# A quarter-block of the output weights in six partitions at a time: one change to a cached grouped-query attention kernel

## The chip, the cores and the metric

The kernel runs on one core of a Trainium2 chip. A core has a matrix engine (TensorE, PE in the profile), three engines for element work (VectorE or DVE, ScalarE or ACT, GpSimd or POOL), a queue engine that here issues nearly all transfers (SyncE, SP), and sixteen DMA engines that move data between the chip's main memory and the on-chip memory SBUF, whose tiles have up to 128 partitions. TensorE writes its products into a second memory, PSUM. The metric is the device time of one execution in microseconds (us), taken as the median of several runs.

## What is computed

One block of attention over a cache, for 8 sequences of 4 new tokens each, 32 query heads that share 8 key/value heads, 2048 cached positions and heads of 128:

```python
q = (x @ wq).reshape(B, Sq, Hq, Dh).transpose(0, 2, 1, 3)
k = jnp.repeat(k_cache, rep, axis=1)
v = jnp.repeat(v_cache, rep, axis=1)
scores = jnp.einsum("bhqd,bhkd->bhqk", q, k) * (Dh ** -0.5)
p = softmax(scores, axis=-1)
o = jnp.einsum("bhqk,bhkd->bhqd", p, v)
return o.transpose(0, 2, 1, 3).reshape(B, Sq, Hq * Dh) @ wo
```

All arrays are bfloat16. The two caches are 32 MB each (8 x 8 x 2048 x 128), wq and wo 4 MB each, x and the result 32 KB.

## The kernel before

**Units and steps.** Two key/value heads of one sequence make a unit: 32 units (`NU`), ordered by head pair `p` (0 to 3) and sequence `b` (0 to 7). A unit's K and V are one transfer of 1 MB each (`load_k` L92, `load_v` L102), 128 partitions with 8 KB in a row. A unit is worked on in two halves, so there are 64 steps (`NH`), and the loop runs ahead by `L` = 6 steps: in one pass it transposes K of the half-unit `step + 7` on TensorE (`transpose_part`, L199), forms the scores of `step + 6` (`scores`, L217) with the exponential on ScalarE (L227), and sums the values of `step` (`values`, L241). At the first half of a unit `norms` sums the exponentials on TensorE (L255), VectorE reduces them and takes the reciprocal (L263, L267); at the second half `finish` multiplies the unit's values by it (L272). The order of every engine's instructions is the order of the program text.

**Projection.** The result needs the product with wo, which is cut into four quarters of 1024 rows, one for each head pair `p`. When a pair is done, `to_tokens(p)` (L284, L290) turns its outputs so that tokens lie in partitions, and `to_wo_rows(p)` (L299, L304) turns them back in the order in which wo lies in SBUF: eight consecutive rows of wo (`WR` = 8) in each of 128 partitions, so that a partition gets 8 KB in a row. For quarters 0 to 2 this happens in the first units of the next pair, quarter 0's in steps 18 and 20. `project(p, r0, n)` (L309) multiplies, `2 n` products of 128 rows by 256 columns, into two PSUM tiles `out_ps`, one for each half of the 512 output columns. Quarter 0 is projected in step 59 (`NH - 5`), after that step's values; the first half of quarter 1 in step 61; the rest after the loop: `to_tokens(3)`, second half of quarter 1, `to_wo_rows(3)`, quarter 2, quarter 3 in three pieces. Then two copies and two stores.

**Loads.** SP issues all loads, in the order of the list `loads`: wq, x, then K of unit `u` and V of unit `u - 3` in turn, with wo's quarter 0 (1 MB) behind V29 and half of quarter 1 (512 KB) behind V30. V31 follows, and behind it the rest of wo in five transfers of 512, 1024, 512, 256 and 256 KB. A load waits for its buffer (7 for K, 6 for V) and for the landing of the load eight places before it, whose semaphore it uses again. `wo_sb` takes the place of `wq_sb`, which is used up by 18 us.

Of the kernel before, what the change touches and what calls it, by code (L numbers as in the profile page):

```python
# [8 lines left out]
BF16 = mybir.dt.bfloat16  # L9
# [5 lines left out]
def kernel(  # L15
# [9 lines left out]
    nc = tc.nc  # L25

    B, Sq, D = x.shape
# [4 lines left out]
    T = B * Sq  # L32
    R = D // 128
    G2 = Hkv // 2
# [3 lines left out]
    HP = 2 * rep  # L38
    scale = float(Dh) ** -0.5
    NU = G2 * B  # L40
    NH = 2 * NU
    KB = 7
    VB = 6
    L = 6
    KA = L // 2 + 1
    WR = HP
    DH = D // 2
# [5 lines left out]
    const = ctx.enter_context(tc.tile_pool(name="const", bufs=1))  # L53
    wpool = ctx.enter_context(tc.tile_pool(name="wpool", bufs=1))
    kpool = ctx.enter_context(tc.tile_pool(name="kpool", bufs=KB))
    vpool = ctx.enter_context(tc.tile_pool(name="vpool", bufs=VB))
# [5 lines left out]
    psum_l = ctx.enter_context(tc.tile_pool(name="psum_l", bufs=1, space=bass.MemoryType.PSUM))  # L62
# [11 lines left out]
    pick = const.tile([128, 2, 2, Dh // 2], BF16, name="pick")  # L74
    ident4 = const.tile([128, 128], FP32, name="ident4")
    oT_all = const.tile([128, Hq, B, Sq], BF16, name="oT_all")
    out_sb = [const.tile([T, DH], BF16, name=f"out_sb{i}") for i in range(2)]
    oP = [const.tile([128, WR, T], BF16, name=f"oP{p}") for p in range(G2)]
    ident = const.tile([128, 128], BF16, name="ident")
    ones = const.tile([128, 128], BF16, name="ones")  # L80
    probs = [const.tile([128, C, NQ], BF16, name=f"probs{i}") for i in range(L // 2 + 2)]
# [15 lines left out]
    def load_v(u):  # L97
# [6 lines left out]
            v_cache[b, 2 * p : 2 * p + 2].rearrange("g (s c) d -> (g s) c d", c=C),  # L104
        )

    def load_wo(p, r0, n):
        rows = wo[p * HP * 128 : (p + 1) * HP * 128, :].rearrange("(q r) j -> q r j", r=WR)
        nc.sync.dma_start(wo_sb[:, p, r0 : r0 + n, :], rows[:, r0 : r0 + n, :])

    nc.sync.dma_start(wq_sb[:, :, :], wq.rearrange("(p r) n -> p r n", r=R))  # L111
    nc.sync.dma_start(x_sb[:, :], x.flatten_outer_dims())  # L112
    loads = []
    for u in range(NU + KA):
        if u < NU:
            loads.append(("k", u))
        if u >= KA - 1 and u - KA + 1 < NU:
            loads.append(("v", u - KA + 1))
        if u in (NU, NU + 1):
            loads.append(("wo", (u - NU, 0, WR if u == NU else 4)))  # L120
    loads.reverse()

    def load_ready(nk, nv):

        while loads:
            kind, u = loads[-1]
            if kind == "wo":
                loads.pop()
                load_wo(*u)
                continue  # L130
            if u >= (nk + KB if kind == "k" else nv + VB):
                return
            loads.pop()
            (load_k if kind == "k" else load_v)(u)

    load_ready(0, 0)

    make_identity(nc, ident[:])
    make_identity(nc, ident4[:])
    for e in range(2):  # L140
        for g in range(2):
            nc.vector.tensor_copy(
                out=pick[:, e, g, :], in_=ident[:, :].rearrange("d (k e) -> d e k", e=2)[:, e, :]
# [2 lines left out]
    nc.vector.memset(ones[:, :], 1.0)  # L146
    for t in probs:
        nc.vector.memset(t[:, :, :], 0.0)

    for r in range(R):  # L150
        xtp = psum_o.tile([128, T], BF16, tag="o", name="xtp")
# [4 lines left out]
    for p in range(G2):  # L156
        psq = psum_s.tile([128, HP, T], FP32, tag="s", name="psq")
        for h in range(HP):
            hh = p * HP + h
            for r in range(R):  # L160
                nc.tensor.matmul(  # L161
                    psq[:, h, :],
                    lhsT=wq_sb[:, r, hh * 128 : (hh + 1) * 128],
                    rhs=xT_sb[:, r, :],
                    start=(r == 0),
                    stop=(r == R - 1),
                )
        nc.scalar.mul(  # L168
            out=qT_all[:, p, :, :, :],
            in_=psq[:, :, :].rearrange("d h (b s) -> d b h s", b=B),  # L170
            mul=scale,
        )
    for p in range(G2):
        pse = psum_s.tile([128, 2, B, NQ], FP32, tag="s", name="pse")
        for e in range(2):
            nc.tensor.matmul(  # L176
                pse[:, e, :, :],
                lhsT=pick[:, e, :, :],
                rhs=qT_all[:, p, :, :, :].rearrange("d b h s -> d (b h s)"),
                start=True,  # L180
                stop=True,
            )
        for g in range(2):
            rows = slice(g * 64, (g + 1) * 64)
            (nc.scalar.copy if g else nc.vector.tensor_copy)(  # L185
                out=q_bd[rows, p, :, :, g, :], in_=pse[rows, :, :, :]
            )

    wo_sb = wpool.tile([128, G2, WR, D], BF16, tag="w", name="wo_sb")
    kt = {}  # L190

    def transpose_part(i, part):
        u, hf = divmod(i, 2)
        c0 = hf * HC + part * (HC // 2)
        kp = psum_k.tile([128, HC // 4, 128], FP32, tag="k", name="kp")
        k4 = ks[u][:, :, :].rearrange("s c d -> s (c d)").bitcast(FP32)
        for j in range(HC // 4):
            w = (c0 // 2 + j) * 128
            nc.tensor.transpose(kp[:, j, :], k4[:, w : w + 128], ident4[:, :])  # L199
        kp2 = kp[:, :, :].rearrange("k j s -> k (j s)").bitcast(BF16)  # L200
        k_t = ktpool.tile([128, HC // 4, 128, 2], BF16, tag="kt", name="kt")
        kt2 = k_t[:, :, :, :].rearrange("k j s e -> k (j s e)")
        if part == 1 and hf == 1:
            nc.scalar.copy(out=kt2, in_=kp2)  # L204
        else:
            nc.vector.tensor_copy(out=kt2, in_=kp2)  # L206
        kt[(i, part)] = k_t

    def scores(i):
        u, hf = divmod(i, 2)  # L210
        p, b = units[u]
        pr = probs[u % len(probs)]
        s_ps = psum_s.tile([128, HC, NQ], FP32, tag="s", name="s_ps")
        for j in range(HC // 2):
            k_t = kt[(i, j // (HC // 4))]
            for e in range(2):
                nc.tensor.matmul(  # L217
                    s_ps[:, 2 * j : 2 * j + 2, :],
                    lhsT=k_t[:, j % (HC // 4), :, e],
                    rhs=q_bd[:, p, e, b, :, :],  # L220
                    start=(e == 0),
                    stop=(e == 1),
                )
        for g in range(2):
            rows = slice(g * 64, (g + 1) * 64)
            cols = slice(g * NQ // 2, (g + 1) * NQ // 2)
            nc.scalar.activation(  # L227
                out=pr[rows, hf * HC : (hf + 1) * HC, cols], in_=s_ps[rows, :, cols], func=EXP
            )
# [21 lines left out]
    def norms(u):  # L251
        pr = probs[u % len(probs)]
        l_ps = psum_l.tile([128, LC, NQ], FP32, tag="l", name="l_ps")
        for c in range(0, C, LC):
            nc.tensor.matmul(  # L255
                l_ps[:, :, :],
                lhsT=ones[:, :],
                rhs=pr[:, c : c + LC, :],
                start=(c == 0),
                stop=(c + LC == C),  # L260
            )
        l_sb = small.tile([128, NQ], FP32, tag="l_sb", name="l_sb")
        nc.vector.tensor_reduce(  # L263
            out=l_sb[:, :], in_=l_ps[:, :, :].rearrange("d c q -> d q c"), axis=AX, op=ADD
        )
        r_sb = small.tile([128, NQ], FP32, tag="r_sb", name="r_sb")
        nc.vector.reciprocal(r_sb[:, :], l_sb[:, :])  # L267
        r_sbs[u] = r_sb
# [10 lines left out]
    nats = {}  # L279
# [14 lines left out]
        nats[p] = nat_sb  # L294

    def to_wo_rows(p):
        perm = psum_l.tile([128, WR, T], BF16, tag="l", name="perm")
        for r in range(WR):
            nc.tensor.transpose(  # L299
                perm[:, r, :],  # L300
                nats[p][:, :, :].rearrange("t q r -> t r q")[:, r, :],
                ident[:T, :T],
            )
        nc.vector.tensor_copy(out=oP[p][:, :, :], in_=perm[:, :, :])  # L304

    def project(p, r0, n):
        for half in range(2):
            for r in range(r0, r0 + n):
                nc.tensor.matmul(  # L309
                    out_ps[half][:, :],  # L310
                    lhsT=oP[p][:, r, :],
                    rhs=wo_sb[:, p, r, half * DH : (half + 1) * DH],
                    start=(p == 0 and r == 0),
                    stop=(p == G2 - 1 and r == WR - 1),
                )

    for step in range(-L - 1, NH):
        i, j = step + L + 1, step + L
        if i < NH:
            transpose_part(i, 0)  # L320
        if 0 <= j < NH:
            scores(j)
        if i < NH:
            transpose_part(i, 1)
        u, hf = divmod(step, 2)
        if step >= 0:
            p, b = units[u]
            if hf == 0:
                norms(u)
            values(step)  # L330
            if hf == 1:
                finish(u)
            elif p > 0 and b == 1:
                to_tokens(p - 1)
            elif p > 0 and b == 2:
                to_wo_rows(p - 1)
        load_ready(min((i + 1) // 2, NU), max((step + 1) // 2, 0))
        if step == NH - 1 - 2 * VB:
            assert not loads
            load_wo(1, 4, 4)  # L340
            load_wo(2, 0, WR)
            load_wo(3, 0, 4)
            load_wo(3, 4, 2)
            load_wo(3, 6, 2)
        if step == NH - 5:
            out_ps = [
                psum_s.tile([T, DH], FP32, tag="s", name=f"out_ps{n}") for n in range(2)
            ]
            project(0, 0, WR)
        elif step == NH - 3:  # L350
            project(1, 0, 4)

    to_tokens(3)
    project(1, 4, 4)
    to_wo_rows(3)
    project(2, 0, WR)
    project(3, 0, 4)
# [37 lines left out]
```

The softmax here doesn't subtract the row's maximum and nothing guards it: scores larger than these inputs give would overflow.

## Time and profile before

| what | value |
|---|---|
| median of 8 runs | 192.63 us (192.37 to 193.01) |
| the profiled execution | 192.61 us |
| its span, first to last instruction | 190.8 us |
| TensorE busy | 153.9 us, 81% |
| VectorE, ScalarE, GpSimd busy | 113.4, 86.2 and 1.1 us |
| read from main memory | 75.53 MB, 396 GB/s over the span |
| K and V transfers, issue to landing | 20.3 us each (median of 32 and 32) |
| projection L309 | 64 products, 7.6 us busy |
| K transposes L199 | 512, 80.6 us busy, 10.9 us idle before them until K landed |

The span leaves out what lies around the program's instructions; 1.8 us here. TensorE's matrix products are pipelined, so a product's own duration (272 ns for L309) is longer than its distance to the next.

### The profile page before, as it was taken

What the parts mean: (1) busy time and instruction counts of PE and PEld (TensorE: products, weight loads), DVE (VectorE), ACT (ScalarE), POOL (GpSimd) and SP (SyncE); (2) the same over time, 40 slices, a digit from 0 to 9 for tenths busy, and PEclk for the clock granted to TensorE, in tenths of its full rate; (3) what the DMA queues carried; (4) which work ended last, traced back from release to release, by engine and by line L of the source; (5) the groups of instructions that cost most, each with busy time, mean ns of one, the idle gap of its engine ahead of it and who ended that gap; (6) DMA issues with size and microseconds to landing.
All of it is one profiled execution on the core that took longest, in us unless ns stands there. A gap on an engine that the chain in (4) does not pass through costs nothing.

```text
span 190.8 us, 6460 instructions
## 1 busy us (share of the span) xinstructions
PE 153.9 (81%) x2892; PEld 139.3 (73%) x2892; DVE 113.4 (59%) x220; ACT 86.2 (45%) x170; POOL 1.1 (1%) x8
## 2 busy tenths in 40 slices
PE   0018867999999999978888889998886999998783
PEld 0007657899999988867778778887775988886572
DVE  6402754677677777756665667676664477673420
ACT  2003665656665654455553444454553555451000
POOL 2000000000000000000000000000000000000000
PEclk9999999999999999999999999999999799999999
DMA  6999999999999999999999999999999999999950
GB/s 220 440 405 421 421 419 417 426 416 419 419 416 417 421 419 417 419 426 412 423 419 423 417 416 417 421 417 424 414 419 421 417 426 416 414 426 411 406 201 9
DMA packets 10539, 75.97 MB, mean 398 GB/s; under 512 B 1200, under 2 KB 1296, under 8 KB 1936
## 3 DMA queue, kind: packets, MB, share of 16 engines
q1 hardware_dynamic: 10464, 75.55, 95.6%
q8 instruction: 22, 0.36, 0.8%
q14 instruction: 5, 0.04, 0.1%
q10 hardware_dynamic: 48, 0.02, 0.0%
HBM read 75.53 MB, written 0.03 MB: 396 GB/s over the span
## 4 chain that ended last, share of the span: by engine, by line
DMA 95%; PE 2%; SPq 1%; issue 0%; ACT 0%
DMA k_sb<-in_k_cache_dram 86%; DMA wo_sb<-in_wo_dram 9%; PE out_ps L309 2%; SPq L92 1%; SPq L112 0%; SPq L111 0%; ACT out_sb L362 0%
## 5 line engine op out<-in xcount | busy, mean ns | idle before, releaser
L199 PE MATMUL kp<-ident,k_sb 128*128 128x128 f32 x512 | 80.6, 283 | 10.9 <-DMA k_sb<-in_k_cache_dram 10.9
L206 DVE COPY kt<-kp 128x1024 bf16<-128x1024 bf16 x96 | 65.2, 684 | 27.9 <-PE kp L199 27.4
L227 ACT ACTIVATE probs<-s_ps 64x256 bf16<-64x256 f32 x128 | 48.3, 378 | 69.6 <-PE s_ps L217 68.9
L199 PEld LDWEIGHTS kp<-ident,k_sb 128*128 128x128 f32 x512 | 54.6, 142 | 12.3 <-issue 11.9
L217 PE MATMUL s_ps<-q_bd,kt 128*128 128x64 bf16 x1024 | 42.8, 194 | 3.4 <-ACT kt L204 2.6
L217 PEld LDWEIGHTS <-kt 128*128 128x128 bf16 x1024 | 40.0, 99 | 5.4 <-ACT kt L204 3.1
L241 PEld LDWEIGHTS <-v_sb 128*128 128x128 bf16 x1024 | 34.5, 96 | 9.4 <-DMA v_sb<-in_v_cache_dram 2.0
L263 DVE TENSOR_REDUCE l_sb<-l_ps 128x32 f32<-128x512 f32 x32 | 22.1, 691 | 23.9 <-PE l_ps L255 23.9
L241 PE MATMUL o_ps<-probs,v_sb 128*128 128x32 bf16 x1024 | 35.1, 177 | 1.0 <-DMA v_sb<-in_v_cache_dram 0.9
L204 ACT COPY kt<-kp 128x1024 bf16<-128x1024 bf16 x32 | 32.4, 1012 | 0.8
L255 PE MATMUL l_ps<-probs,ones 128*128 128x512 bf16 x64 | 19.1, 379 | 0.0
L267 DVE RECIPROCAL r_sb<-l_sb 128x32 f32<-128x32 f32 x32 | 11.3, 353 | 1.1
L152 PE MATMUL xtp<-ident,x_sb 32*128 32x32 bf16 x4 | 0.5, 189 | 13.6 <-DMA x_sb<-in_x_dram 13.4
L152 PEld LDWEIGHTS <-x_sb 32*128 32x128 bf16 x4 | 0.3, 113 | 13.7 <-DMA x_sb<-in_x_dram 13.4
L309 PE MATMUL out_ps<-wo_sb,oP 128*32 128x256 bf16 x64 | 7.6, 272 | 1.2 <-DMA wo_sb<-in_wo_dram 1.2
L168 ACT ACTIVATE qT_all<-psq 128x256 bf16<-128x256 f32 x4 | 1.5, 383 | 14.7 <-PE psq L161 14.7
L309 PEld LDWEIGHTS <-oP 128*32 128x32 bf16 x64 | 6.1, 96 | 1.9 <-issue 1.1
L362 ACT CAST out_sb<-out_ps 32x256 bf16<-32x256 f32 x1 | 0.4, 362 | 15.0 <-PE out_ps L309 15.0
L272 DVE TENSOR_TENSOR oT_all<-o_ps,r_sb 128x32 bf16<-128x32 f32 x32 | 5.8, 182 | 1.7 <-PE o_ps L241 1.5
L255 PEld LDWEIGHTS <-ones 128*128 128x128 bf16 x64 | 6.0, 98 | 0.8 <-issue 0.4
L185 DVE CAST q_bd<-pse 64x512 bf16<-64x512 f32 x4 | 2.6, 683 | 4.2 <-PE pse L176 4.2
L155 DVE COPY xT_sb<-xtp 128x32 bf16<-128x32 bf16 x4 | 0.5, 168 | 6.9 <-PE xtp L152 6.9
(23 smaller groups left out, 33.3 us busy)
## 6 DMA issues: line engine op xcount, KB each, us to landing
k_sb<-in_k_cache_dram SPq DMA_DIRECT2D x32, 1024.0 KB, 20.3
v_sb<-in_v_cache_dram SPq DMA_DIRECT2D x32, 1024.0 KB, 20.3
wq_sb<-in_wq_dram SPq DMA_DIRECT2D x1, 4096.0 KB, 12.4
wo_sb<-in_wo_dram SPq DMA_DIRECT2D x2, 1024.0 KB, 18.9
wo_sb<-in_wo_dram SPq DMA_DIRECT2D x3, 512.0 KB, 17.4
wo_sb<-in_wo_dram SPq DMA_DIRECT2D x2, 256.0 KB, 13.4
x_sb<-in_x_dram SPq DMA_DIRECT2D x1, 32.0 KB, 12.2
out_dram<-out_sb SPq DMA_DIRECT2D x1, 16.0 KB, 1.4
```

Of the source, the lines that this page charges most:

```text
L185: (nc.scalar.copy if g else nc.vector.tensor_copy)(out=q_bd[rows, p, :, :, g, :], in_=pse[rows, :, :, :])
L199: nc.tensor.transpose(kp[:, j, :], k4[:, w : w + 128], ident4[:, :])
L204: nc.scalar.copy(out=kt2, in_=kp2)
L206: nc.vector.tensor_copy(out=kt2, in_=kp2)
L217: nc.tensor.matmul(s_ps[:, 2 * j : 2 * j + 2, :], lhsT=k_t[:, j % (HC // 4), :, e], rhs=q_bd[:, p, e, b, :, :], start=(e == 0), stop=(e == 1),
L227: nc.scalar.activation(out=pr[rows, hf * HC : (hf + 1) * HC, cols], in_=s_ps[rows, :, cols], func=EXP)
L241: nc.tensor.matmul(o_ps[u][:, :], lhsT=vs[u][:, cc, :], rhs=pr[:, cc, :], start=(cc == 0), stop=(cc == C - 1),)
L255: nc.tensor.matmul(l_ps[:, :, :], lhsT=ones[:, :], rhs=pr[:, c : c + LC, :], start=(c == 0), stop=(c + LC == C),)
L263: nc.vector.tensor_reduce(out=l_sb[:, :], in_=l_ps[:, :, :].rearrange("d c q -> d q c"), axis=AX, op=ADD)
L267: nc.vector.reciprocal(r_sb[:, :], l_sb[:, :])
L272: nc.vector.tensor_tensor(out=oT_all[:, p * HP : (p + 1) * HP, b, :], in0=o_ps[u][:, :].rearrange("d (h s) -> d h s", h=HP), in1=r_sbs[u][ ...
L309: nc.tensor.matmul(out_ps[half][:, :], lhsT=oP[p][:, r, :], rhs=wo_sb[:, p, r, half * DH : (half + 1) * DH], start=(p == 0 and r == 0), st ...
```

## The change

768 of the 1024 rows of wo's quarter 0 are laid out anew: sixteen consecutive rows (16 KB) in each of 48 partitions, namely 0 to 23 and 32 to 55 of a 64-partition tile `wo_e`. They are loaded by eight transfers, each to six partitions that lie four apart, one transfer behind the K and V blocks issued for units 8 to 15. The other 256 rows lie two to a partition in a tile `wo_m`, one transfer of 256 KB at the place of the old 1 MB transfer. Partitions 24 to 31 and 56 to 63 of `wo_e` are set to zero by GpSimd at the start, as is the whole tile.

`to_wo_rows(0)` makes 34 transposes in place of 8 (two groups of 32 partitions for each of sixteen rows, and two of 128) and two copies in place of one. `project(0)` makes 18 products for each half of the output columns in place of 8: sixteen over 64 partitions, two over 128. The two halves are taken apart: columns 0 to 255 in step 58, the others in step 59, each after the step's values.

```diff
+    NE, WE, WM = 48, 16, 2
+    wo_e = const.tile([64, WE, D], BF16, name="wo_e")
+    wo_m = const.tile([128, WM, D], BF16, name="wo_m")
+    oE = const.tile([64, WE, T], BF16, name="oE")
+    oM = const.tile([128, WM, T], BF16, name="oM")
...
+    def load_wo_e(i):
+        hi, m = divmod(i, 4)
+        rows = wo[: NE * WE, :].rearrange("(q r) j -> q r j", r=WE)
+        a, b = hi * 32 + m, hi * NE // 2 + m
+        nc.sync.dma_start(wo_e[a : a + 21 : 4, :, :], rows[b : b + 21 : 4, :, :])
+
+    def load_wo_m():
+        nc.sync.dma_start(
+            wo_m[:, :, :], wo[NE * WE : HP * 128, :].rearrange("(q r) j -> q r j", r=WM)
+        )
...
-        if u in (NU, NU + 1):
-            loads.append(("wo", (u - NU, 0, WR if u == NU else 4)))
+        if 8 <= u < 16:
+            loads.append(("e", u - 8))
+        if u == NU:
+            loads.append(("m", 0))
+        if u == NU + 1:
+            loads.append(("wo", 0))
...
+    nc.gpsimd.memset(wo_e[:, :, :], 0.0)
...
+        perm = psum_l.tile([128, WE + WM, T], BF16, tag="l", name="perm")
+        rows = flat.rearrange("t (q r) -> t r q", r=WE)
+        for r in range(WE):
+            for hi in range(2):
+                q0 = hi * NE // 2
+                nc.tensor.transpose(
+                    perm[hi * 32 : hi * 32 + 32, r, :], rows[:, r, q0 : q0 + 32], ident[:T, :T]
+                )
+        rows = flat[:, NE * WE :].rearrange("t (q r) -> t r q", r=WM)
+        for r in range(WM):
+            nc.tensor.transpose(perm[:, WE + r, :], rows[:, r, :], ident[:T, :T])
+        nc.vector.tensor_copy(out=oE[:, :, :], in_=perm[:64, :WE, :])
+        nc.vector.tensor_copy(out=oM[:, :, :], in_=perm[:, WE:, :])
...
+    def project(p, r0, n, halves=(0, 1)):
+        for half in halves:
+            cols = slice(half * DH, (half + 1) * DH)
+            if p == 0:
+                parts = [(oE[:, r, :], wo_e[:, r, cols]) for r in range(WE)]
+                parts += [(oM[:, r, :], wo_m[:, r, cols]) for r in range(WM)]
...
-        if step == NH - 5:
+        if step == NH - 6:
             out_ps = [
                 psum_s.tile([T, DH], FP32, tag="s", name=f"out_ps{n}") for n in range(2)
             ]
-            project(0, 0, WR)
+            project(0, 0, WR, (0,))
+        elif step == NH - 5:
+            project(0, 0, WR, (1,))
```

`wo_sb` now holds quarters 1 to 3 only; their loads and products are as before.

More of the change, by code (lines that the diff above doesn't have):

```diff
@@ L41 @@
     NH = 2 * NU
+    NE, WE, WM = 48, 16, 2
+    assert NE * WE + 128 * WM == HP * 128
     KB = 7
@@ L76 @@
     oT_all = const.tile([128, Hq, B, Sq], BF16, name="oT_all")
+    wo_e = const.tile([64, WE, D], BF16, name="wo_e")
+    wo_m = const.tile([128, WM, D], BF16, name="wo_m")
     out_sb = [const.tile([T, DH], BF16, name=f"out_sb{i}") for i in range(2)]
-    oP = [const.tile([128, WR, T], BF16, name=f"oP{p}") for p in range(G2)]
+    oP = [None] + [const.tile([128, WR, T], BF16, name=f"oP{p}") for p in range(1, G2)]
+    oE = const.tile([64, WE, T], BF16, name="oE")
+    oM = const.tile([128, WM, T], BF16, name="oM")
     ident = const.tile([128, 128], BF16, name="ident")
@@ L105, in load_v @@
         )
+    def load_wo_e(i):
[7 more added lines that the diff above has]
+        )
     def load_wo(p, r0, n):
         rows = wo[p * HP * 128 : (p + 1) * HP * 128, :].rearrange("(q r) j -> q r j", r=WR)
-        nc.sync.dma_start(wo_sb[:, p, r0 : r0 + n, :], rows[:, r0 : r0 + n, :])
+        nc.sync.dma_start(wo_sb[:, p - 1, r0 : r0 + n, :], rows[:, r0 : r0 + n, :])
     nc.sync.dma_start(wq_sb[:, :, :], wq.rearrange("(p r) n -> p r n", r=R))
@@ L126, in load_ready @@
             kind, u = loads[-1]
-            if kind == "wo":
+            if kind in "e m wo":
                 loads.pop()
-                load_wo(*u)
+                if kind == "e":
+                    load_wo_e(u)
+                elif kind == "m":
+                    load_wo_m()
+                else:
+                    load_wo(1, 0, 4)
                 continue
@@ L187 @@
             )
-    wo_sb = wpool.tile([128, G2, WR, D], BF16, tag="w", name="wo_sb")
+    wo_sb = wpool.tile([128, G2 - 1, WR, D], BF16, tag="w", name="wo_sb")
     kt = {}
@@ L296, in to_wo_rows @@
     def to_wo_rows(p):
[L297 to L308, printed above, removed]
+        flat = nats[p][:, :, :].rearrange("t q r -> t (q r)")
@@ new lines, in to_wo_rows @@
+        if p > 0:
+            perm = psum_l.tile([128, WR, T], BF16, tag="l", name="perm")
+            rows = flat.rearrange("t (q r) -> t r q", r=WR)
+            for r in range(WR):
+                nc.tensor.transpose(perm[:, r, :], rows[:, r, :], ident[:T, :T])
+            nc.vector.tensor_copy(out=oP[p][:, :, :], in_=perm[:, :, :])
+            return
+        perm = psum_l.tile([128, WE + WM, T], BF16, tag="l", name="perm")
[6 more added lines that the diff above has]
+                )
@@ new lines, in to_wo_rows @@
+        rows = flat[:, NE * WE :].rearrange("t (q r) -> t r q", r=WM)
[9 more added lines that the diff above has]
+                parts += [(oM[:, r, :], wo_m[:, r, cols]) for r in range(WM)]
+            else:
+                parts = [(oP[p][:, r, :], wo_sb[:, p - 1, r, cols]) for r in range(r0, r0 + n)]
+            for i, (o, w) in enumerate(parts):
@@ L309, in project @@
                 nc.tensor.matmul(
                     out_ps[half][:, :],
[L311 to L314, printed above, removed]
+                    lhsT=o,
+                    rhs=w,
+                    start=(p == 0 and i == 0),
+                    stop=(p == G2 - 1 and r0 + i == WR - 1),
                 )
```

## The prediction

> **What bounds the kernel now.** I read the page first: the DMA rows, the queues, the chain of waits.
>
> ```profile
> DMA  6999999999999999999999999999999999999950
> GB/s 220 440 405 421 421 419 417 426 416 419 419 416 417 421 419 417 419 426 412 423 419 423 417 416 417 421 417 424 414 419 421 417 426 416 414 426 411 406 201 9
> q1 hardware_dynamic: 10464, 75.55, 95.6%
> q8 instruction: 22, 0.36, 0.8%
> q14 instruction: 5, 0.04, 0.1%
> DMA 95%; PE 2%; SPq 1%; issue 0%; ACT 0%
> ```
>
> The sixteen DMA engines are full from start to end and the chain that ended last is 95% DMA. Two things follow. Fewer bytes in front of the last transfers would bring them sooner. And the last busy slice (181 to 186 us) is only half full: the engines do not finish together. The 22 + 5 instruction packets of 16 and 8 KB are the only traffic that is not spread evenly.
>
> How uneven the engines are stands in the trace's landing records. A transfer raises its semaphore sixteen times, once for each engine's share. Sorted, in us from the span's start, for the last K block (unit 31), the last V block and the last piece of wo:
>
> ```
> K31  161.65 .68 .69 .75 .93 162.47 .51 163.62 164.72 .94 .95 .99 165.10 166.18 .27 166.77
> V31  175.31 .33 .36 .43 .58 176.16 .85 177.31 178.43 .62 .64 179.86 .97 180.22 .32 180.46
> wo   181.66 .67 .72 .80 .89 182.48 183.14 .56 184.68 .88 186.10 .22 .44 .47 .57 186.69
> ```
>
> The earliest and the last engine are 5.0 us apart at the end (0.6 us at the first K block). Five engines lie within 0.25 us; a sixth is 0.82 late, two more 1.5 and 1.9, eight 3.0 to 5.0. The late ones slip by about 1.5 us at a time, each time just after a 16 KB instruction packet (one at 39.50 us, a landing 1.52 us further behind at 42.10). So there is slack on a few engines, but a transfer counts as landed only with the last of the sixteen.
>
> Then the timeline from the last K block on, where the end is made:
>
> ```profile
> 166.91 0.63 PE L199 MATMUL kp<-ident,k_sb 128*128 128x128 f32 x4 [0.31 <-DMA k_sb<-in_k_cache_dram]
> 172.36 0.59 PE L255 MATMUL l_ps<-probs,ones 128*128 128x512 bf16 x2
> 172.79 0.95 PE L241 MATMUL o_ps<-probs,v_sb 128*128 128x32 bf16 x32
> 174.25 1.91 PE L309 MATMUL out_ps<-wo_sb,oP 128*32 128x256 bf16 x16 [0.51 <-DMA wo_sb<-in_wo_dram]
> 176.08 0.61 PE L255 MATMUL l_ps<-probs,ones 128*128 128x512 bf16 x2
> 176.74 0.96 PE L241 MATMUL o_ps<-probs,v_sb 128*128 128x32 bf16 x32
> 178.01 1.03 PE L309 MATMUL out_ps<-wo_sb,oP 128*32 128x256 bf16 x8 [0.30 <-DMA wo_sb<-in_wo_dram]
> 178.97 0.61 PE L255 MATMUL l_ps<-probs,ones 128*128 128x512 bf16 x2
> 180.34 0.35 DVE L267 RECIPROCAL r_sb<-l_sb 128x32 f32<-128x32 f32 x1
> 180.50 0.96 PE L241 MATMUL o_ps<-probs,v_sb 128*128 128x32 bf16 x32 [0.93 <-DMA v_sb<-in_v_cache_dram]
> 181.51 0.19 DVE L272 TENSOR_TENSOR oT_all<-o_ps,r_sb 128x32 bf16<-128x32 f32 x1 [0.81 <-PE o_ps L241]
> 183.18 0.66 PE L299 MATMUL perm<-ident,nat_sb 32*128 32x32 bf16 x8
> 184.20 3.65 PE L309 MATMUL out_ps<-wo_sb,oP 128*32 128x256 bf16 x32 [0.35 <-DMA wo_sb<-in_wo_dram]
> ```
>
> TensorE starts K31 at 166.91, just after its last share (166.77), and from there waits for DMA only in small pieces. By what would follow directly: 0.51 before the first projection, 0.23 before the values at 176.74, 0.29 before the second projection, 1.10 before the last values, 0.36 before the last 32 products, together 2.49 us. That is all the slack TensorE has between K31 and the end.
>
> **The change part by part.** (1) *Eight transfers of 96 KB* (six partitions of 16 KB) go to SP's queue between the K blocks of units 8 to 15, and the 1 MB transfer of wo's first quarter behind V29 becomes 256 KB. Price of a share: the 32 KB packets of wq took 1.213 us each, so 16 KB is 0.607 and with its 4-byte semaphore packet (0.009 to 0.011) 0.62; eight are 4.94 us on an engine that carries one share of each. The trace of before has no transfer of six partitions. From below, six shares over all sixteen engines are 0.23 us a transfer, 1.85 for eight; from above, all on one engine, 3.7 and 29.6. Every 128-partition transfer here goes as one packet a partition, evenly over the engines, so one share to each of six engines is nearest, and I take 4.94. [...] Which of the lags above belong to these six, the profile does not say: it numbers no engine.
>
> (2) *What the other ten gain.* They lose 48 KB of the 64 KB that the old transfer gave each. A 1 MB transfer is 2.48 us on every engine (K31 and V29 in the first column, 161.65 and 166.62, are two apart), so 48 KB are 1.86 us. The six pay 4.94 - 1.86 = 3.08 net. If they are the six earliest, the last landing moves from 5.03 behind the earliest to the later of 5.03 - 1.86 = 3.17 and 0.82 + 3.08 = 3.90: 1.13 us sooner. That is the whole possible gain on the DMA side, for V31 and the last wo too.
>
> (3) *But K31 comes before the gain.* The removed bytes lay behind V29, which is behind K31. So the ten keep their K31 times (last 166.77), while the six come 4.94 later: the five earliest at 166.6 to 166.9, the sixth at 162.47 + 4.94 = 167.41. K31 lands 0.64 later. Queued behind it on TensorE is the whole rest of the program.
>
> (4) *Projection of quarter 0*: 36 products instead of 16. Sixteen took 174.25 to 176.08, 0.1144 each; twenty more are 2.29 us. They are half as high, but rows of this trace give nothing for height: the 32-row transposes at 183.18 need 0.08 each, like the 128-row ones of L284 (0.61 for eight). [...]
>
> (5) *The tail replayed* on before's clock with no DMA wait: norms 172.36, values of step 58 172.79 to 173.27, half 0 to 175.33, values of step 59 to 175.81, half 1 to 177.87, norms, values 178.30 to 179.27, eight products to 180.23, norms at 180.23. V31 (sixth engine 176.16 + 3.08 = 179.24, late ones 180.46 - 1.86 = 178.60) is in by then, so the last values need no wait and end at 181.63. The multiply of L272 also needs the reciprocal, which ended 1.72 after the norms began (178.97 to 180.69): 181.95. It starts 0.46 later than before (181.51). From there to the last 32 products nothing changes but the 0.36 wait for wo, which is gone: +0.10. So 2.29 of work went into 2.49 of waiting, 0.10 to the bad because the reciprocal now ends last.
>
> (6) *At nothing*: 26 more transposes and one more copy in step 20 (26 at 0.083 = 2.2 us, copy under 0.7). TensorE waits 10.9 us for K over 32 units, 0.34 a unit, and eleven units to K22 take it up; without that cover it is 2.9 us. The memset of wo_e on POOL: 128 columns took 0.20, one column 0.10, so 8192 are about 6.6 us by 9 us; x lands at 13.36 and SP's first small transfer goes out after 30. If it held VectorE's own memsets, they would still end at 12.6. Eight more issues on SP, 0.33 each: SP waits about 148 us for landings in all, and a block lands 20.3 us after its issue, eight times 2.48, so eight transfers are in flight; the small ones take places there, leaving 5.3 of 8 MB, 13 us of work per engine, so no engine runs dry; the K and V behind them wait only for places.
>
> **Sum.** 192.61 (span 190.8 and 1.8 around it; the median is 192.63, 0.02 more) + 0.64 + 0.10 = 193.35; on the median 193.4.
>
> **Rivals.** *The sixth engine is not late* (its one 0.65 us slip, after an 8 KB instruction packet at 132.13, falls elsewhere, or a share is cheaper): K31 moves by 0 to 0.1, the end by 0.1 to 0.2, 192.75: no measurable change. [...] Against: it is in every landing since 137 us. *The DMA gain comes through* because TensorE isn't the bound: then 192.63 - 1.13 = 191.5, faster. It needs the twenty products nearly free; under 1.2 us for all twenty (2.29 less 0.74 and 0.39) the end is measurably sooner, under 0.42 the whole 1.13 comes. Against: (4). *Shares spread, or a 1.9 us engine among the six*: K31 later by 1.85 (16 engines) or 163.62 + 4.94 - 166.77 = 1.8: 194.5. *The six are late engines*: K31 at 164.72 + 4.94 up to 166.77 + 4.94, 2.9 to 4.9 later: 195.6 to 197.7. [...] That the small transfers all run on one engine (over 210 us) gets 1%.
>
> **How the numbers follow.** Forecast 50% (192.9 or rather 193.1 to 193.8), no change 20%, faster 10% (191.4 to 192.2), 194.5 9%, late engines 11%. The range 192.3 to 194.7 holds the first, the second and the fourth, 79%. Under 0.2% (0.39 us) a measurement of this kernel cannot tell from no change: faster 0.10, same 0.20, slower 0.70.
>
> **What would show it.** Right: landings of the last wo about 1.1 us sooner, yet K31's last share near 167.4; no DMA wait at the projection lines after K31; 36 products of 0.114; the reciprocal, not V31, ahead of the last multiply. Wrong: K31 at 166.8 (first rival), products under 0.08 each or waits for V31 left (second), K31 past 168.5 (third and fourth).

## The result, and the profile after

The median went from 192.6 us (30 runs, 192.37 to 193.01) to 195.2 us (11 runs, 193.86 to 196.02): a ratio of 1.0116 [1.0101, 1.0132], 2.6 us slower. The eleven times lie in two groups, five at 193.86 to 194.44 and six at 195.20 to 196.02; the median is the lowest of the upper six. The profiled execution belongs to the upper group: 195.46 us, span 193.7. Two executions of the experiments, the profiled one of run 1 (197.25 us) and one of run 7 (196.19 us), lie over 1.5% above the fastest of the same kernel and are left out of the medians and ranges given there.

The profile after: first the DMA rows, then the queues (packets, MB, share of 16 engines' span), then the chain that ended last by engine and by line:

```profile
DMA  6999999999999999999999999999999999999500
GB/s 217 433 415 426 418 430 426 426 425 418 426 423 423 423 426 423 423 428 423 428 425 418 430 423 426 420 421 423 430 423 426 423 428 423 418 422 401 208 19 7
q1 hardware_dynamic: 10560, 75.55, 93.2%
q8 instruction: 23, 0.38, 0.7%
DMA 71%; PE 20%; DVE 3%; ACT 3%; issue 1%; SPq 0%; DVEq 0%
DMA k_sb<-in_k_cache_dram 49%; DMA v_sb<-in_v_cache_dram 8%; DMA wo_e<-in_wo_dram 7%; DMA x_sb<-in_x_dram 6%; PE out_ps L359 5%; PE kp L229 4%; PE s_ps L247 3%; PE o_ps L271 2%; PE psq L191 2%; ACT kt L234 2%; PE l_ps L285 1%; DVE l_sb L293 1%; DVE q_bd L215 1%; DVE kt L236 1%; ACT probs L257 1%
```

Before, DMA was 95% of the chain, to the end. Now it is 71%, with the small transfers (`wo_e`) in it by name, and TensorE holds 20%: the last stage. The DMA row is empty in the last two slices (of 4.8 us), where before it was one. And the rates are a little higher: mostly 418 to 430 where before they were 414 to 426. The last point is easily passed over; it turned out to be worth nearly as much as the loss.

The waits of TensorE for transfers, in us in total, times, longest:

```profile
PE kp L229 <- DMA k_sb<-in_k_cache_dram: 12.2, 14, 2.6
```

Apart from the start (x), this is the only one left. The waits for V and for wo after K31 are gone, as the forecast said. So everything turns on when K31 lands. The timeline from there (start, length; gaps of the engine in brackets):

```profile
169.46 0.63 PE L229 MATMUL kp<-ident,k_sb 128*128 128x128 f32 x4
...
175.82 1.92 PE L359 MATMUL out_ps<-wo_e,oE 64*32 64x256 bf16 x16
177.67 0.11 PEld L359 LDWEIGHTS <-oM 128*32 128x32 bf16 x2 [0.21 <-issue]
177.67 0.39 PE L359 MATMUL out_ps<-wo_m,oM 128*32 128x256 bf16 x2
178.00 0.56 PE L271 MATMUL o_ps<-probs,v_sb 128*128 128x32 bf16 x16
178.49 1.92 PE L359 MATMUL out_ps<-wo_e,oE 64*32 64x256 bf16 x16
180.34 0.39 PE L359 MATMUL out_ps<-wo_m,oM 128*32 128x256 bf16 x2
180.66 0.60 PE L285 MATMUL l_ps<-probs,ones 128*128 128x512 bf16 x2
...
183.41 0.95 PE L271 MATMUL o_ps<-probs,v_sb 128*128 128x32 bf16 x32
184.34 0.35 DVE L297 RECIPROCAL r_sb<-l_sb 128x32 f32<-128x32 f32 x1
184.79 0.19 DVE L302 TENSOR_TENSOR oT_all<-o_ps,r_sb 128x32 bf16<-128x32 f32 x1
187.07 3.67 PE L359 MATMUL out_ps<-wo_sb,oP 128*32 128x256 bf16 x32
```

K31 starts at 169.46 where before it was 166.91. The last 32 products start at 187.07 instead of 184.20. Of these 2.87 us, 2.56 are K31's landing and 0.31 is the stretch behind it. The landing records of K31, sorted, say where the 2.56 come from (us from the span's start, one for each of the sixteen engines):

```
before  161.65 .68 .69 .75 .93 162.47 .51 163.62 164.72 .94 .95 .99 165.10 166.18 .27 166.77
after   159.92 160.11 .38 162.73 .86 163.06 .20 .22 164.20 .35 .66 .82 165.46 .58 166.41 169.33
```

Fifteen engines have landed by 166.41, before the old time. One comes 2.92 us after all others. It alone holds TensorE.

### The profile page after: what moved, and what is told of

Its sections match the earlier page's. It is cut to its first block, busy times and chain, and to the rows that moved or that the text cites. A ratio compares the mean times of both kernels' runs of the same rounds, so it can differ in the third digit from the quotient of the medians.

```text
span 193.7 us, 6563 instructions
## 1 busy us (share of the span) xinstructions
PE 157.0 (81%) x2938; PEld 141.5 (73%) x2938; DVE 116.4 (60%) x221; ACT 86.2 (45%) x170; POOL 8.0 (4%) x9
## 4 chain that ended last, share of the span: by engine, by line
DMA 71%; PE 20%; DVE 3%; ACT 3%; issue 1%; SPq 0%; DVEq 0%
DMA k_sb<-in_k_cache_dram 49%; DMA v_sb<-in_v_cache_dram 8%; DMA wo_e<-in_wo_dram 7%; DMA x_sb<-in_x_dram 6%; PE out_ps L359 5%; PE kp L229 4%; PE s_ps L247 3%; PE o_ps L271 2%; PE psq L191 2%; ACT kt L234 2%; PE l_ps L285 1%; DVE l_sb L293 1%; DVE q_bd L215 1%; DVE kt L236 1%; ACT probs L257 1%
## 5 line engine op out<-in xcount | busy, mean ns | idle before, releaser
L171 DVE COPY pick<-ident 128x64 bf16<-128x64 bf16 x4 | 7.4, 1922 | 1.3 <-POOL ident masks.py:199 1.3
L178 POOL MEMSET wo_e<- 64x8192 bf16 x1 | 7.0, 6963 | 0.0
L359 PE MATMUL out_ps<-wo_sb,oP 128*32 128x256 bf16 x48 | 5.8, 273 | 0.0
```

The costliest lines, as they stand in the source:

```text
L171: nc.vector.tensor_copy(out=pick[:, e, g, :], in_=ident[:, :].rearrange("d (k e) -> d e k", e=2)[:, e, :])
L178: nc.gpsimd.memset(wo_e[:, :, :], 0.0)
L359: nc.tensor.matmul(out_ps[half][:, :], lhsT=o, rhs=w, start=(p == 0 and i == 0), stop=(p == G2 - 1 and r0 + i == WR - 1),)
```

## The experiments

Where the expectations name theories by letter, A is the one held after this reading: the landing sum of the forecast is right, but one of the six engines that carry the small transfers is a late one. B and C, its rivals, look for the loss elsewhere than in which engines are loaded; D came up after run 4: the new tiles move the K and V buffers to other addresses. Each "before" is the kernel before, timed on the same chip beside the run. The first profile is the one of the result above.

**1. The changed kernel again**, unchanged.

> The changed kernel once more, unchanged. Theory A (one of the six engines that carry the small transfers is one of the eight that instruction packets make late): the profile again shows five of the six landing together and the sixth some 2 to 3 us behind, K31 lands near 169.3 and the time is 195 to 196; where the late engines fall otherwise, K31 lands near 167.4 and the time is about 194. Rival B (a share of a small transfer costs more than 0.62 us): all six are equally late. Rival C (the added work of TensorE costs it): K31 at 166.8 to 167.4 in the slow profile too.

195.27 us (194.28 to 195.39), 1.0119 [1.0088, 1.0149] of before. The profiled execution (197.25) is late from the first blocks on (K8 landed at 50.27 to 52.17, in the first profile at 46.95 to 48.76). K31 landed at 171.11, and one engine came last in it again, but 1.45 behind the next and not 2 to 3. The 16 KB packets of the small transfers took 0.611 us each, as in the first profile, which leaves B without support. The last product ended 21.42 us after K31's last landing; in the first profile it was 21.41 (169.33 to 190.74), and 21.41 too in runs 3, 4, 9, 10 and 11, which have the same 36 products. In all of these TensorE waits for no transfer behind K31 (run 6 has such a wait).

**2. Which engines are late: probes in the kernel before.** Behind each K and V issued from unit 22 on, a transfer of 512 bytes to each of `k` partitions, `k` = 1, 2, 3 and so on up to 15:

```diff
+    probe = const.tile([16, 16, 256], BF16, name="probe")
...
+        nc.sync.dma_start(probe[:k, k, :], wo[:k, :256])
```

> The kernel before with fifteen transfers of 1 to 15 partitions with 512 bytes each, one behind each K and V block from K22 on; nothing else changed. Theory A: a transfer of k partitions lands on k engines, always the same first ones, so the landing that a probe has more than the one before it tells the lag of one more engine. Among the first six there is exactly one that lies 3 us or more behind the earliest, seven of the other ten are late too. Rival (the first six are all early): probes 1 to 6 land within 0.9 us of the earliest engine. Time unchanged within 0.5 us of 192.6 by both.

192.74 us against 192.67: the probes cost nothing that shows. Besides one record at its issue, a transfer to `k` partitions landed in `k` steps. Their lags behind the earliest are those of `k` - 1, to 0.4 us (but for the one slip told below), and one more, so the set of engines is read as that of `k` - 1 and one more:

```
k=4  124.56 125.12 125.35 126.72
k=5  127.12 127.14 127.72 127.87 129.19
k=6  129.58 129.60 130.30 130.39 131.69 132.73
k=7  132.34 132.53 132.85 132.92 133.87 134.20 135.13
k=8  134.63 134.65 135.35 135.42 135.49 136.72 137.65 137.93
```

Numbering the engines in the order in which the probes add them, the new one at `k` = 6, engine 5, is 3.15 us behind the earliest. The new one at `k` = 7, engine 6, is 1.53 behind (133.87); a 16 KB instruction packet at 133.79 sets it back, and at `k` = 8 it is the last (137.93), while the new one, engine 7, is early. Followed to `k` = 15 the list gives engines 0, 1, 2, 4, 7 and 8 as early, by elimination 15 too, 3 in the middle (about 2.1 behind at V20), and 5, 6 and 9 to 14 as the eight late ones: one among the first six, as theory A had it. Six partitions load engines 0 to 5: five that have slack or some of it (0 to 2.11 us behind the earliest at `k` = 6), and one late one (3.15).

**3. The small transfers left out**, so that 768 rows of quarter 0 are missing (everything else of the change kept):

```diff
-        if 8 <= u < 16:
-            loads.append(("e", u - 8))
```

> The changed kernel without its eight small transfers: 768 rows of wo's quarter 0 are left out (those partitions stay zero), all products are made. Theory A: K31 lands near 166.8 as before, V31 and the last wo 1.9 us sooner than before, but TensorE has no slack after K31, so the end lies 21.4 us behind K31 as in the changed kernel: 192.9 to 193.1. If the end were set by the transfers: 190.8. Rival C (the added work costs the 2.6 us): 195. So this tells whether the small transfers or the work make the loss.

190.64 us (190.49 to 190.79), 0.9893 [0.9879, 0.9908]: not back to before but 2 us under it. The timeline of this kernel, K31 and the last 32 products:

```profile
164.49 0.63 PE L227 MATMUL kp<-ident,k_sb 128*128 128x128 f32 x4 [0.15 <-DMA k_sb<-in_k_cache_dram]
...
182.10 3.67 PE L357 MATMUL out_ps<-wo_sb,oP 128*32 128x256 bf16 x32
```

The expected K31 was missed by 2.4 us, and the expected time by more than 2: K31 landed at 164.35 (sixteen records from 159.78 to 164.35), not 166.8. Two things follow. The eight shares cost 169.33 - 164.35 = 4.98 us at K31, 0.62 each (a share's packet took 0.611, the semaphore packet behind it 0.009). And something else in the change *saves* 166.77 - 164.35 = 2.42. It is not fewer bytes, since nothing that the kernel before loads ahead of K31 was removed. What differs all along is the pace. The windows view gives for two stretches their limits, length, busy time of PE, PEld, DVE, ACT and POOL, granted clock, DMA share and GB/s; before:

```profile
60.00:100.00 40.00, 35.43 (x691) 32.44 (x688) 27.06 (x52) 21.46 (x42) 0.00 (x0) 1.00 1.01 419
100.00:120.00 20.00, 17.24 (x336) 15.88 (x336) 12.92 (x25) 9.54 (x21) 0.00 (x0) 1.00 1.01 419
```

and after:

```profile
100.00:120.00 20.00, 17.54 (x348) 16.08 (x346) 13.54 (x26) 10.09 (x20) 0.00 (x0) 1.00 1.01 425
```

With the same DMA share (full), 425 GB/s instead of 419: each packet is faster. The trace's 8 KB packets took 314.5 ns in the mean before (5 to 95%: 309 to 321) and 310.5 after (309 to 309). The new tiles, less the one that they replace, take 19,072 bytes of each partition, and the buffers behind them move: in the compiled program K's start at 77,696 before, 128 over a multiple of 256, and at 96,768 after, a multiple of 256; V's go from 135,040 to 154,112, likewise.

**4. The same rows in one block of 48 partitions**, so that all sixteen engines share each transfer:

```diff
-        nc.sync.dma_start(wo_e[a : a + 21 : 4, :, :], rows[b : b + 21 : 4, :, :])
+        nc.sync.dma_start(wo_e[:NE, 2 * i : 2 * i + 2, :], rows[:, 2 * i : 2 * i + 2, :])
...
-                q0 = hi * NE // 2
+                q0 = hi * 32
```

> The changed kernel with its 768 rows in partitions 0 to 47 in a row, loaded by eight transfers of 96 KB over all 48 partitions (two rows each) at the same places, so that all sixteen engines carry 6 KB of each in place of six engines 16 KB; work of TensorE as in the changed kernel. Theory A: every engine is 1.9 us later at K31, K31 lands near 168.6, time 194.5 to 194.9, with no second group of times. Rival B: 195.5 or more. If K31's landing did not matter: 193.0.

196.99 us (196.5 to 197.12), 1.0218 [1.0201, 1.0236], a miss: spreading made it worse than the change, and the time is the one that B had. K31 landed at 170.98 where 168.6 was expected:

```profile
171.11 0.63 PE L227 MATMUL kp<-ident,k_sb 128*128 128x128 f32 x4 [0.32 <-DMA k_sb<-in_k_cache_dram]
...
188.72 3.67 PE L357 MATMUL out_ps<-wo_sb,oP 128*32 128x256 bf16 x32
```

From the first landing of K8 to that of K16 it took 45.7 us against 39.3 without the transfers (run 3): 6.4 for eight, 0.80 each on every engine, where 1/16 of 96 KB at the pace of the other loads is 0.23. The transfers' own packets are not what was dear (2 KB, 84 ns in the median, the same in run 8). The 8 KB packets of K and V beside them were: 343 ns in the mean between 45 and 95 us, where the change has 311 and this run itself 310 behind it. That is 4.5 us on each engine, and with 1.9 for the bytes it makes the 6.4. What makes it so is taken up in runs 8 and 11.

**5. The kernel before with 128 bytes more in each partition in front of its buffers**, and nothing else:

```diff
+    pad = const.tile([128, 64], BF16, name="pad")
```

> The kernel before with one unused tile of 128 bytes a partition ahead of the others, nothing else: it moves the K and V buffers from addresses that are 128 over a multiple of 256 bytes to multiples of 256, where the changed kernel happens to have them. Theory D (the address sets the pace of the K and V packets): packets of 8 KB go from a mean of 314 to 310 ns, a unit's K and V from 4.97 to 4.91 us on every engine, K31 lands at 164.4 instead of 166.8, time 190.0 to 190.5. Rival (the faster pace of the changed kernel has another source, such as the small transfers or the chip): 192.6.

190.12 us (190.02 to 190.30), 0.9872 [0.9857, 0.9886] of before. K31 landed at 164.44, as in run 3. The rate in the stretch shown above:

```profile
60.00:100.00 40.00, 35.49 (x691) 33.04 (x698) 27.22 (x52) 21.62 (x43) 0.00 (x0) 1.00 1.01 424
```

Theory D holds: an unused tile of 128 bytes a partition gives 2.5 us, and the change had this gain hidden in it. In the compiled programs of runs 2 and 6 the K and V buffers start 128 over a multiple of 256 as well, and their 8 KB packets took 315 and 314 ns; in runs 3, 5, 7 and 8 they start at multiples, and it was 310 to 311. The pad moves every tile behind it; no run moved K and V alone, and no offset but 128 was tried. The end of this kernel looks like that of before, only sooner, with its small waits:

```profile
171.93 1.91 PE L310 MATMUL out_ps<-wo_sb,oP 128*32 128x256 bf16 x16 [0.52 <-DMA wo_sb<-in_wo_dram]
...
178.05 0.96 PE L242 MATMUL o_ps<-probs,v_sb 128*128 128x32 bf16 x32 [0.88 <-DMA v_sb<-in_v_cache_dram]
...
181.89 3.65 PE L310 MATMUL out_ps<-wo_sb,oP 128*32 128x256 bf16 x32 [0.50 <-DMA wo_sb<-in_wo_dram]
```

**6. The changed kernel with the same pad**, which takes its gain away again.

> The changed kernel with the same unused tile of 128 bytes, which moves its K and V buffers off the multiples of 256. Theory D: 2.4 us slower than the changed kernel, 196.5 to 198.2, K31 2.4 later. Rival: 195.3, unchanged.

196.14 us (195.95 to 196.49), 1.0185 [1.017, 1.0201]: just under the range expected. Packets are back at 314.4 ns in the mean. K31 landed at 169.66, less than the expected sum, because engine 5 had been set back twice and not three times by then (it comes 1.15 behind the next engine, as in run 9). Beside the two executions of the change of which that is also true (runs 9 and 10), K31 is 1.84 later (169.66 against 167.82) and the profiled execution 2.35 longer (196.33 against 193.98). The other 0.5 is a wait behind K31: the third slip came before V29 landed (176.14), and TensorE had to wait for it.

```profile
176.19 0.56 PE L272 MATMUL o_ps<-probs,v_sb 128*128 128x32 bf16 x16 [0.57 <-DMA v_sb<-in_v_cache_dram]
```

**7. Five engines**: 40 partitions instead of 48, five in each transfer, so that engine 5 carries none; `wo_m` three rows a partition, and a pad that keeps the addresses.

```diff
-    NE, WE, WM = 48, 16, 2
+    NE, WE, WM = 40, 16, 3
...
-        nc.sync.dma_start(wo_e[a : a + 21 : 4, :, :], rows[b : b + 21 : 4, :, :])
+        nc.sync.dma_start(wo_e[a : a + 17 : 4, :, :], rows[b : b + 17 : 4, :, :])
```

> The changed kernel with five partitions in each small transfer in place of six (640 rows in 40 partitions, the other 384 rows three to a partition; K and V buffers at multiples of 256 as there; 38 products in place of 36). Theory A (the sixth loaded engine, which instruction packets make late, sets K31): K31 is then set by the fourth engine, which in the changed kernel's trace comes second last, 166.0 to 166.8, and the end follows 21.4 + 0.2 later: 192.6 to 193.3, without the spread of the changed kernel's times. Rival B (small transfers delay K31 whichever engines carry them): 195 and more.

193.01 us (192.77 to 193.06); 1.0022 [1.0012, 1.0032]. A hit in time and in K31 (166.42):

```profile
166.56 0.63 PE L230 MATMUL kp<-ident,k_sb 128*128 128x128 f32 x4 [0.22 <-DMA k_sb<-in_k_cache_dram]
...
184.37 3.67 PE L360 MATMUL out_ps<-wo_sb,oP 128*32 128x256 bf16 x32
```

Leaving out one engine moves K31 from 169.33 to 166.42, the place that the other fifteen engines had in the change (166.41). The second group of times is gone with it: nine executions lie within 0.3 us.

**8. The same bytes over 128 partitions**: six rows in each, three transfers of 256 KB behind K8, K11 and K14, eight products a half, addresses kept.

```diff
-    NE, WE, WM = 48, 16, 2
+    NE, WE, WM = 128, 6, 2
...
+        nc.sync.dma_start(wo_e[:, 2 * i : 2 * i + 2, :], rows[:, 2 * i : 2 * i + 2, :])
...
-        if 8 <= u < 16:
-            loads.append(("e", u - 8))
+        if u in (8, 11, 14):
+            loads.append(("e", (u - 8) // 3))
```

> The changed kernel with its 768 rows over all 128 partitions (six rows each, three transfers of 256 KB at K8, K11 and K14), so that all engines carry the same, each to its own partitions, and the projection needs 8 products a half; K and V at multiples of 256. Theory A: K31 2.0 later than without early bytes, 166.4, but TensorE has its slack back, so the last V sets the end: 190.5 to 191.0. If early bytes cost in themselves, as the run over 48 partitions had it (0.80 us a transfer on every engine): K31 near 170, 195 or more.

190.15 us (190.05 to 190.28), 0.9873 [0.9858, 0.9887]. K31 landed at 166.37, 1.93 after run 5's, close to the 1.85 of even shares: so neither spreading over all engines nor moving early made run 4 dear, nor its packets of 2 KB, which are the same here. Yet the time is that of run 5, less than expected:

```profile
166.50 0.63 PE L227 MATMUL kp<-ident,k_sb 128*128 128x128 f32 x4 [0.51 <-DMA k_sb<-in_k_cache_dram]
...
178.08 0.86 PEld L269 LDWEIGHTS <-v_sb 128*128 128x128 bf16 x32 [0.35 <-DMA v_sb<-in_v_cache_dram]
178.08 0.96 PE L269 MATMUL o_ps<-probs,v_sb 128*128 128x32 bf16 x32
179.70 0.62 PE L312 MATMUL nat<-ident,oT_all 128*32 128x128 bf16 x8 [0.65 <-DVE oT_all L300]
...
181.79 3.65 PE L353 MATMUL out_ps<-wo_sb,oP 128*32 128x256 bf16 x32
```

With sixteen products, as before, TensorE has its slack behind K31, and 1.93 of delay vanish in it. V31 sets the end: the last values start at 178.08, just behind its landing at 178.04, and their weight load waits 0.35 for it (in run 5 it landed at 178.00, and TensorE waited 0.88). The bytes ahead of V31 are the same wherever they lie.

**9 and 10. The changed kernel twice more**, one profiled execution each, to see both groups of times.

> The changed kernel once more, unchanged, for another profile. Theory A with its refinement (instruction packets of 16 KB go to eight engines in turn, and where the turn starts differs from execution to execution): the time is near 194.1 or near 195.3. Near 194.1, engine 5 (the one of the six that is late) must show its third slip after K31 and K31 must land 1.4 to 1.5 sooner than in the changed kernel's first profile, 167.8 to 168.0; near 195.3 before K31 and K31 at 169.3. In both the last product ends 21.4 after K31.

> As the run before it: a further profile of the changed kernel, for the same reading.

193.99 and 193.96 us, both of the lower group; before there 192.78. Run 9:

```profile
167.97 0.63 PE L229 MATMUL kp<-ident,k_sb 128*128 128x128 f32 x4 [0.19 <-DMA k_sb<-in_k_cache_dram]
...
185.58 3.67 PE L359 MATMUL out_ps<-wo_sb,oP 128*32 128x256 bf16 x32
```

K31 lands at 167.83 and 167.81, 1.5 sooner than in the first profile, and the time is 1.5 less. The distance between engine 5 and the next engine tells why. In the first profile it was 1.49 at K27 and 3.04 at K28, a slip just before, by the instruction packet at 149.47. In runs 9 and 10 it was 1.15 and 1.35 at K31, and 2.68 and 2.89 at V31, 13 us later. The same slip comes before K31 in the one group and behind it in the other. The packets tell why it is this engine. In the first profile 88% of the 8 KB packets of loads between 60 and 160 us start 3 ns before another packet ends, and so the packets of one engine can be followed. In the first profile six engines have the 16 KB shares, and only one of them takes 16 KB instruction packets as well: at 30.4, 86.7 and 149.5 us. These are eight packets apart (0.882, 0.881 and 0.879 us long), and so it is on the other engines (the packets next behind these three: 0.879, 0.879 and 0.886 us): the instruction packets went to the eight late engines in turn. In run 10 engine 5 takes them at 59.7 and 118.5, and the next one of its turn comes at 177.9, behind K31. So where the turn begins differs between executions. What sets its beginning was not tried.

**11. Run 4 with the reads in order**: each transfer takes 96 consecutive rows of wo, the writes stay in partitions 0 to 47.

```diff
+        rows = wo[2 * NE * i : 2 * NE * (i + 1), :].rearrange("(q r) j -> q r j", r=2)
+        nc.sync.dma_start(wo_e[:NE, 2 * i : 2 * i + 2, :], rows[:, :, :])
...
```

> The run over 48 partitions again, with the rows of each transfer consecutive in memory (96 rows, two to a partition) in place of two rows out of every sixteen; the tile, the partitions, the engines and the work are the same. If the stride of the reads made each of those transfers cost 0.80 us on every engine: 0.23 us each, K31 at 166.4, time 192.5 to 193. If it is the writing, sixteen engines into 48 partitions: K31 at 171 and 197 again.

196.92 us (one execution), K31 at 170.69: as dear as run 4, and the K and V packets between 45 and 95 us took 342 ns. So the stride of the reads is not the cause, and the side that is written is what is left to suspect. Sixteen engines into 48 partitions were dear (K31 at 170.98 and 170.69) and into 128 (run 8, 166.37) were not; but run 8 also has three transfers in place of eight, so the cause is not shown.

## Why the prediction was wrong

The profiled execution, put together from measured terms: 192.61 - 2.42 (addresses) + 4.98 (eight shares on engine 5) + 0.31 (the stretch from K31 to the end) = 195.48; measured 195.46. It closes because the terms are read from the same traces; what tests them are runs 3, 5 and 7. The forecast had 0.64 for the first two together and 0.10 for the third.

- **(0) What bounds it.** Held. After K31 TensorE has 2.49 us of slack: run 8 hid 1.93 in it; the change, which uses it up, hides nothing.
- **(1) The price of a share.** Held: six landings, 0.62 us on one engine each (4.98 for eight).
- **(2) and (3) Which engines.** This is the step that failed: "five earliest at 166.6 to 166.9, the sixth at 162.47 + 4.94 = 167.41" took the six for the six earliest. One of them, engine 5, is a late one, and K31 landed at 169.33. Engine 3, the one in the middle, is among the six too and comes second last (166.41), which is the third rival's case hidden behind the fourth's. The fourth rival (late engines, 195.6 to 197.7, 11%) names what happened, at one engine in place of several. Its price was an addition to the old K31, as the forecast's was, and so without the 2.42. Whether the six are late ones the profile did not say, as it numbers none: by run 2 the late ones are 5, 6 and 9 to 14. The 1.13 us for the last landings, which needed six early engines, did not come either: V31 landed at 181.05 and the last wo at 187.26, where before it was 180.46 and 186.69.
- **Not in the sum at all: the addresses.** The parts of the change were its instructions and transfers; that the new tiles move every buffer behind them was not costed. Its 2.42 us came by luck and hid half of the loss. A packet of 8 KB took 314.5 ns before and 310.5 after, 1.3% less; why the start of the buffers sets this, no run shows.
- **(4) Twenty more products.** Held in the main: sixteen of half height took 175.82 to 177.67, 0.1156 each, no cheaper than full ones. Missed was a gap of about 0.1 us in each half where TensorE goes from 64 rows to 128 (the 0.21 in brackets at 177.67): a half took 2.18 and 2.17, not 18 × 0.1144 = 2.06.
- **(5) The tail.** The order held, with the reciprocal (184.34 to 184.69) ahead of the last multiply at 184.79 and no wait for a transfer. The size did not: 0.31 instead of 0.10, and the 0.2 between them are the longer halves of (4). (181.95 is 0.44 behind 181.51, not 0.46; the 0.10 should have been 0.08.)
- **(6) At nothing.** Held. GpSimd's memset took 6.96 us and ended at 8.7; beside it VectorE's four small copies took 7.43 us in all, where before they took 0.62, but that was over long before x landed. The lines, before and then after:

```profile
1.33 0.62 DVE L142 COPY pick<-ident 128x64 bf16<-128x64 bf16 x4 [1.33 <-POOL ident masks.py:199]
1.33 7.43 DVE L171 COPY pick<-ident 128x64 bf16<-128x64 bf16 x4 [1.33 <-POOL ident masks.py:199]
1.75 6.96 POOL L178 MEMSET wo_e<- 64x8192 bf16 x1
```

The sign was right, slower, and the size too small. Against run 5, which has the same addresses without the change, the loss is 195.2 - 190.12 = 5.1 us for the median, 4.0 for the lower group. Runs 5 and 8 are quicker than both kernels, and neither needs the layout in 48 partitions; run 8 shows that the early place of the bytes was not the fault, only the choice of six partitions and the products that they ask for.

## What to carry to other kernels

With all DMA engines full, as here, a transfer to few partitions was paid by the engines it lands on (0.62 us for a share of 16 KB), and the price was set by the latest of them (K31 at 169.33, where the other fifteen had landed by 166.41): before loading "idle" engines, find out with small nested probes which ones they are. A new tile is also a shift of every tile behind it (here by 19,072 bytes, worth 2.42 us): compare the addresses of the large buffers before and after, and run a pad by itself, before the difference in time is put down to the work. What transfers gain or lose is to be set against the slack of the engine that comes after them: TensorE's 2.49 us hid 1.93 of later landing in run 8, and the change, whose twenty more products fill them, hid nothing.

## What the runs showed of the hardware that was not expected

- 128 bytes in the start of the buffers: 419 against 424 GB/s and 192.6 against 190.1 us (before and run 5); between before and the change, which differ in more than that, 8 KB packets of 314.5 against 310.5 ns and 16 KB instruction packets of 1,076 against 935 ns (means).
- Eight of the sixteen engines served the 16 KB instruction packets in turn, and each packet set its engine back by some 1.5 us (in the change 1.49 to 3.04 behind the next engine, from K27 to K28), which it did not make up: before, eight engines end 3.0 to 5.0 behind the earliest. The turn began differently between executions, and the changed kernel, whose last landing hung on one of them, had two times, 1.5 us apart (195.46 in the first profile, 193.99 and 193.96 in runs 9 and 10).
- Transfers of 96 KB by sixteen engines into 48 partitions (run 4) cost every engine 0.80 us each, against 0.23 estimated from the pace of the other loads; most of it was in the K and V packets beside them (343 against 311 ns).
